# Second gated MLP: the first block product copied by ScalarE into a second PSUM bank, and new due times for the planner

## The chip, the cores and the metric

The kernel runs on one core of a Trainium2 chip. The metric is the device time of one execution in microseconds. Of three runs of the kernel before, the median is 1006.6 us (1005.06 to 1008.88); the execution that was profiled took 1006.01 us, with a span of 1004.2 us from its first to its last instruction.

## The reference, cut to what matters

Attention over 4 batches of 576 tokens with 8 heads of 64 (half of the heads see a plain window of 32, half a dilated one) is followed by two gated MLPs on 2304 tokens, 512 wide inside and 1536 in the middle:

```python
def _moe_ref(x, w_gate, w_val, w_out, rms_g):        # first MLP
    xn = x / np.sqrt(np.mean(x * x, -1, keepdims=True) + 1e-06) * rms_g
    g = xn @ w_gate
    return g * (1.0 / (1.0 + np.exp(-g))) * (xn @ w_val) @ w_out

def _moe2_ref(x, w_gate, w_val, w_out):              # second MLP
    gate = 1.0 / (1.0 + np.exp(-(x @ w_gate)))
    return gate * (x @ w_val) @ w_out
```

## The kernel before, in words

Every fp32 product is made of three passes of TensorE on a high and a low part of each operand (high by high, high by low, low by high); `split` (line 578) makes the parts: a cast on ScalarE, a subtraction on GpSimd or VectorE.

The order of all work is planned in Python while the kernel is built. `add` enters an operation with its engine (or engines, each other one at a penalty from `PARAMS`), its cost, what it reads and writes, its tiles and a due time. `Line.emit` then plays the engines forward: each engine takes the operation that can begin first, and among those that can begin at once the one with the smallest due time. A tile of a ring (a PSUM bank, a buffer) can be taken when its last user has ended. Each engine then runs its list in the order found. Products of the two MLPs carry the key `PE order`, so TensorE keeps the order in which they were entered; what the planner chooses for them is the time. The due times come from `PARAMS`: `att0`, `span0` and `lo1` to `hi5` for the attention groups, `turn0` and `turn1` for the first transposes, `wdue` and `wslope` for the weights of the first MLP, and so on.

Stages: attention of the first tokens, then chunks of 384 tokens of the first MLP in which the remaining attention is interleaved (to about 280 us of the profile), the rest of the first MLP (to about 588 us), the second MLP, and the output.

The second MLP (`half`, `unit`, `y_products`) multiplies 2x2 blocks with seven block products in place of eight (Winograd's form): four blocks of the result, named 11, 12, 21, 22, are sums of seven products. Three passes hold four of the twelve column groups each; a pass goes over four batches, a batch over two units, a unit has a gate half and a value half: 24 units, 48 halves, seven products of six matmuls each. In a half, product 0 goes to bank X and ScalarE copies it to SBUF as block 11 (`snap`, line 1595); product 1 goes to Y and is copied as block 22; product 2 is added by TensorE onto X and copied as block 12; product 3 is added onto Y and VectorE adds Y to 12 (`plus`, line 1601); product 4 is added onto X, and VectorE adds X to 22; product 5 goes to bank Z and VectorE adds Z to 11; product 6 is added onto X, which then is block 21. `finish` (line 1607) takes a tanh of a gate block on ScalarE (line 1612) or multiplies a value block by its gate on VectorE (line 1624). Block 21 is read from its bank, the other three from SBUF. The two halves of a unit take turns product by product.

Banks: X takes `g`, `v` and `y3` in turn; Y and Z take the two banks `att`. The output products of the batch before (`y_products`, line 1487) are put between, at places given by `y_from` and `y_step` (`y_last` in the last batch but one); their X is `y0` or `y1` in turn, Y and Z are `y2`. Each ends in an addition on VectorE (line 1463). Outputs go out through transposes on VectorE (line 1560) and four DMAs each (line 1567); the last two pairs of blocks through transposes on TensorE into `g` and `v` (line 1539), copies on ScalarE (line 1544) and DMAs (line 1551).

Of the kernel before, what the change touches and what calls it, by code (L numbers as in the profile page):

```python
# [8 lines left out]
F32 = mybir.dt.float32  # L9
# [15 lines left out]
    "late": 0, "fill_share": -1.519, "fill_max": 6, "gather": 0.866, "w0_hi": 17.594,  # L25
    "w0_lo": 13.068, "h0_hi": 0.512, "h0_lo": -0.096, "x0_hi": 0.96, "x0_lo": 1.138, "ahead": 2,
    "todo0": 464.368, "todo1": 9.635, "todo2": 47.212, "todo3": 0.618, "xb_zero": -1.082,
    "stay": 0.104, "phase": 1.6, "fill_from": 7.028, "fill_gap": -3.039, "margin": 2139.515,
    "wait": 1.172, "w_sq": 3.146, "w_hi": 0.024, "w_lo": 0.907, "x_hi": 0.265, "x_lo": 0.0,
    "h_hi": 7.774, "h_lo": 0.002, "qk": 0.304, "norm": 0.51, "pts": 8.696, "o": 0.0, "snap": 6.738,  # L30
    "h_ahead": 8.667, "h2_ahead": 0.956, "evac": 7.026, "holds": (6, 6), "norm_act": 1.016,
    "slack": 0.0, "share_v": 0.6, "share_p": 0.33, "cold": 1.7, "low": 0, "high": 0.39,
    "recip": 0.3, "rel1": 106.122, "span1": -0.902, "rel2": 17.835, "span2": -0.521, "ys": 0.468,
    "ts": 0.415, "cross": 0.06, "same": 0.04, "dma_lat": 1.7, "dma_rate": 330000.0, "by_pe": 0,
# [3 lines left out]
    "ld_v": -61.445, "ld_c": -66.281, "ld_d": -14.37, "lead": 1.181, "xdue": 12.095,  # L38
    "wdue": -1.028, "wslope": 2.786, "wload": -341.212, "wload_step": 9.03, "warm_n": 36,
    "warm_t": 0.889, "warm_dt": 0.03, "warm_c": 19, "warm_m": 5, "warm_late": -3.526,  # L40
    "warm_due": 32.425, "mask_cost": 0.18, "exp_cost": 0.36, "s_cost": 0.546, "o_cost": 0.41,
    "t_cost": 0.265, "pt_lead": 8.027, "x_lead": 12.171, "wy_due": -0.031, "y_from": 7.985,
    "y_step": 1.502, "xb_due": 0.362, "y_last": 1.346, "xb_last": 6.045, "lo6": 114.359,
    "hi6": 18.752, "sizes": (384, 384, 384, 384, 384, 384), "wide": (384, 384, 384, 384, 384, 384),
    "rush": -0.629, "rush_to": 0.301,
# [296 lines left out]
def attention_then_two_gated_mlps(  # L342
# [103 lines left out]
    def act(n):  # L446
        return 0.09 + n / 1190
# [589 lines left out]
    def x_norm(c, due, banks):  # L1037
        T1 = SIZES[c]
        R = T1 // TT
        sq = new("sb", "pt", [P, KD, T1], F32, 2)  # L1040
# [72 lines left out]
        xo = [new("sb", "xo", [P, 2, 2, T1], F32R, NX) for _ in range(2)]  # L1113
        rbp = new("ps", banks[1], [P, TT, R], F32, 2 if banks[1] == "att" else 1)

        def turn():
# [3 lines left out]
        add("PE", 0.247, turn, reads=[("rb", c), "ident"], writes=[("rbp", c), "x order"],  # L1120
            tiles=[rb, rbp] + xo, due=due, lat=0.08, cols=3 * R, fill=filler(rbp))
        xtile[0, c] = xo
        for kk in range(KD):
# [14 lines left out]
            if L2P > ONE:  # L1138
                dma(lambda kk=kk, xn=xn: nc.sync.dma_start(out=xf_scr[c][:, kk], in_=xn.t),
                    512.0 * T1, reads=[("xn", c, kk)], writes=[("xf", c, kk)], tiles=[xn],  # L1140
                    due=due + 12)
        for k in range(2):
# [154 lines left out]
    def mlp_step(p, c, f, s):  # L1297
# [11 lines left out]
        def proj(which, bank, due):  # L1309
            def products(ks):  # L1310
                for kk in ks:
# [3 lines left out]
                    for n, (l, r) in enumerate(((0, 0), (0, 1), (1, 0))):  # L1315
# [3 lines left out]
                                         start=kk == 0 and n == 0, stop=kk == KD - 1 and n == 2)  # L1319

            alone = (p, c, f, which) == (0, 0, 0, 0)
            for ks in [[kk] for kk in range(KD)] if alone else [list(range(KD))]:
# [6 lines left out]
                    cols=3 * T1 * len(ks), fill=filler(bank) if ks[0] == 0 else None)  # L1329

        proj(0, gb, s)
        if p:
            add("ACT", act(T1), lambda: nc.scalar.activation(out=t.t, in_=gb.t, func=ACTF.Silu),
                reads=[("bank", p, c, f, 0)], writes=[key], tiles=[gb, t], due=s + 1.9 * mul)
        else:
# [8 lines left out]
            writes=[key], tiles=[vb, t], due=s + 3.7 * mul)  # L1344
# [523 lines left out]
```

## Time and profile before

| | |
|---|---|
| median of three runs | 1006.6 us (1005.06 to 1008.88) |
| the profiled execution | 1006.01 us, span 1004.2 us |
| TensorE busy | 977.1 us, 97% of the span |
| VectorE busy | 732.2 us, 73% |
| ScalarE busy | 477.8 us, 48% |
| GpSimd busy | 406.3 us, 40% |
| mean granted TensorE clock | 0.975 of full |
| HBM | 129.5 MB read, 63.7 MB written |

How to read it: PE is TensorE's matmuls, PEld its weight loads, DVE VectorE, ACT ScalarE, POOL GpSimd, SP the engine that issues DMAs. A granted clock of 1.00 is 2.4 GHz, 0.50 is 1.2 GHz. A busy TensorE with clock 1.00 in a long stretch is a stretch that is bound by its own products; what can be won or lost there are gaps. The idle time named for a group is that of its engine just before it, with what ended the wait.

### The profile page before, as it was taken

To read this page: it belongs to the slowest core of one execution; us is meant where nothing else is said; L and a number is where in the kernel's file an instruction comes from. 1 tells how busy PE (TensorE), PEld (TensorE's weight loads), DVE (VectorE), ACT (ScalarE), POOL (GpSimd) and SP (SyncE) were. 2 spreads that over 40 slices of the span, in tenths; PEclk is the share of its full clock that TensorE was granted. 3 is DMA by queue.
4 is the path that set the end of the run, shared out by engine and by line. 5 is a ranking of instruction groups with operands and counts; after the bars stand their busy time and mean duration, and the time that the engine had idled before them with its cause. 6 is when DMAs were issued, how large, how long until landed. Compare 5 with 4: busy or idle time off the path is not lost. (4 is left out here: it accounts for less than half of the span.)

```text
span 1004.2 us, 20084 instructions
## 1 busy us (share of the span) xinstructions
PE 977.1 (97%) x7096; PEld 947.2 (94%) x7096; DVE 732.2 (73%) x1712; ACT 477.8 (48%) x1305; POOL 406.3 (40%) x602
## 2 busy tenths in 40 slices
PE   7899899999999999999999999999999999999997
PEld 6688798998999999999999999999999999999996
DVE  6778897868895888733432579788977688787765
ACT  5876657647442542322221345646654446454432
POOL 5653874444342730010000467337852047651111
PEclk8769799999999999999999999999999999999998
DMA  9858698676779587966563354645176454547634
GB/s 203 190 154 178 136 287 218 156 201 198 250 226 364 193 285 236 345 204 219 214 216 101 107 168 180 237 166 184 66 255 224 155 199 147 202 134 217 160 85 87
DMA packets 213253, 194.53 MB, mean 194 GB/s; under 512 B 137313, under 2 KB 178849, under 8 KB 213153
## 3 DMA queue, kind: packets, MB, share of 16 engines
q1 hardware_dynamic: 213152, 193.25, 63.5%
q8 instruction: 56, 0.92, 0.4%
q14 instruction: 45, 0.36, 0.1%
HBM read 129.50 MB, written 63.70 MB: 192 GB/s over the span
## 5 line engine op out<-in xcount | busy, mean ns | idle before, releaser
L1368 PE MATMUL y<-h,wo 128*128 128x384 f32 x864 | 166.5, 338 | 0.5 <-DVE h L588 0.4
L1318 PE MATMUL g<-xo,w 128*128 128x384 f32 x864 | 165.9, 340 | 0.0
L1318 PE MATMUL v<-xo,w 128*128 128x384 f32 x864 | 163.0, 336 | 0.0
L1318 PEld LDWEIGHTS g<-xo,w 128*128 128x128 f32 x864 | 152.2, 191 | 0.4 <-issue 0.2
L1368 PEld LDWEIGHTS y<-h,wo 128*128 128x128 f32 x864 | 149.3, 188 | 2.4 <-DVE h L588 0.7
L1318 PEld LDWEIGHTS v<-xo,w 128*128 128x128 f32 x864 | 150.4, 188 | 1.3
L581 ACT CAST h<-t 128x384 fp32r<-128x384 f32 (+1 forms) x139 | 65.8, 473 | 116.7 <-DVE t L1342 87.3
L585 POOL TENSOR_TENSOR h<-t,h 128x288 fp32r<-128x288 f32 (+1 forms) x45 | 42.8, 953 | 159.3 <-ACT h L581 153.4
L1463 DVE SCALAR_TENSOR_TENSOR pt<-y,pt 128x288 f32<-128x288 f32 x136 | 61.3, 451 | 37.2 <-PE y L1510 34.5
L1342 DVE TENSOR_TENSOR t<-t,v 128x384 f32<-128x384 f32 x72 | 39.6, 549 | 66.0 <-PE v L1318 65.4
L972 POOL TENSOR_SCALAR pr<-pr,rs 128x96 f32<-128x96 f32 x132 | 57.0, 445 | 57.0 <-DVE rs L967 39.5
L1510 PE MATMUL y<-h,wo 128*128 128x288 f32 x408 | 75.0, 298 | 0.1
L588 DVE TENSOR_TENSOR h<-t,h 128x384 fp32r<-128x384 f32 (+1 forms) x95 | 58.8, 619 | 20.5 <-ACT h L581 19.6
L585 POOL TENSOR_TENSOR w<-wz,w 128x256 fp32r<-128x256 f32 x58 | 47.5, 833 | 46.3 <-ACT w L581 32.9
L562 ACT ACTIVATE wz<-wst 128x512 f32<-128x512 f32 x72 | 48.0, 670 | 33.4 <-DMA z<-wz 21.5
L1510 PEld LDWEIGHTS y<-h,wo 128*128 128x128 f32 x408 | 61.4, 190 | 0.8 <-DVE pt L1463 0.3
L585 POOL TENSOR_TENSOR w<-S,w 128x256 fp32r<-128x256 f32 x48 | 38.7, 820 | 52.1 <-DVE w L583 38.0
L571 DVE SCALAR_TENSOR_TENSOR wz<-wst,wz 128x512 int32<-128x512 int32 x72 | 56.6, 787 | 0.9
L959 ACT ACTIVATE pr<-pr,nmx 128x96 f32<-128x96 f32 x144 | 52.4, 365 | 9.2 <-DVE nmx L953 8.9
L574 DVE SCALAR_TENSOR_TENSOR wz<-wst,wz 128x512 int32<-128x512 int32 x72 | 52.8, 734 | 0.6
L1612 ACT ACTIVATE t<-t 128x288 f32<-128x288 f32 x72 | 31.9, 444 | 44.7 <-DVE t L1603 43.2
L585 POOL TENSOR_TENSOR x<-t,x 128x288 fp32r<-128x288 f32 x29 | 27.2, 940 | 63.0 <-ACT x L581 62.9
(224 smaller groups left out, 2111.4 us busy)
## 6 DMA issues: line engine op xcount, KB each, us to landing
z<-wz SPq DMA_DIRECT2D x54, 256.0 KB, 4.4
xo<-xs SPq DMA_DIRECT2D x23, 576.0 KB, 5.8
wst<-in_moe_w_gate_dram SPq DMA_DIRECT2D x24, 512.0 KB, 4.6
wst<-in_moe_w_val_dram SPq DMA_DIRECT2D x24, 512.0 KB, 5.1
wst<-in_moe_w_out_dram SPq DMA_DIRECT2D x24, 512.0 KB, 5.5
xs<-xs SPq DMA_DIRECT2D x21, 576.0 KB, 2.8
wst<-xs SPq DMA_DIRECT2D x18, 576.0 KB, 5.4
x<-xo SPq DMA_DIRECT2D x24, 384.0 KB, 3.2
```

The lines of the kernel that those rows point to most:

```text
L562: add("ACT", act(CW), lambda: nc.scalar.activation(out=z.t.bitcast(F32), in_=top().bitcast(F32), func=ACTF.Abs), reads=[("wst", key)], wri ...
L571: add("DVE", Shared(0.595), lambda: nc.vector.scalar_tensor_tensor(out=z.t, in0=top(), scalar=-0x40000000, in1=z.t, op0=ALU.bitwise_and, o ...
L574: add("DVE", Shared(0.595), lambda: nc.vector.scalar_tensor_tensor(out=z.t, in0=low(), scalar=29, in1=z.t, op0=ALU.logical_shift_right, op ...
L581: add("ACT", act(n), lambda: nc.scalar.copy(out=hi(), in_=src()), reads=reads, writes=[key] + [order] * bool(order), tiles=tiles + [dst], ...
L585: add("PL", pool(n), lambda: nc.gpsimd.tensor_tensor(out=lo(), in0=src(), in1=hi().bitcast(F32), op=ALU.subtract), reads=reads, writes=[ke ...
L588: other=(kind + "_lo", "DVE", dves(n), lambda: nc.vector.tensor_tensor(out=lo(), in0=src(), in1=hi().bitcast(F32), op=ALU.subtract)))
L959: add("ACT", PARAMS["exp_cost"], lambda u=u: nc.scalar.activation(out=pr.t[:, u], in_=pr.t[:, u], func=ACTF.Exp, bias=nmx.t[:, u:u + 1], s ...
L972: add("PL", Shared(0.305), lambda u=u: nc.gpsimd.tensor_scalar(out=pr.t[:, u], in0=pr.t[:, u], scalar1=rs.t[:, u:u + 1], scalar2=1.0, op0= ...
L1318: nc.tensor.matmul(out=bank.t, lhsT=w[:, l, cols], rhs=x, start=kk == 0 and n == 0, stop=kk == KD - 1 and n == 2)
L1368: nc.tensor.matmul(out=yb.t, lhsT=w.t[:, l, s], rhs=hs[r].t if broad(p, c) else hs[r].t[:, r], start=n == 0 and j == 0, stop=n == HOLDS[p] ...
L1463: add("DVE", dve(T), lambda: nc.vector.scalar_tensor_tensor(out=t.t[:, e, h], in0=bank.t, scalar=0.5, in1=t.t[:, e, h], op0=ALU.mult, op1= ...
L1510: nc.tensor.matmul(out=bank.t, lhsT=w.t[:, u, a, n], rhs=hs[u].t[:, d], start=first and u == 0 and m == 0, stop=u == NF // 2 - 1 and m == ...
```

## The change

In each half of the second MLP, `fork` copies product 0 from X into bank Z (ScalarE, PSUM to PSUM) where `snap` had copied it to SBUF, and product 5 is added by TensorE onto Z. Block 11 is then complete in Z and is read from there; the addition `plus("11", ...)` on VectorE is gone. Product 6 (block 21) is now made ahead of product 5 (block 11), in the halves and in the output products. Banks: X and Z are `g` and `y0` in the gate half, `v` and `y1` in the value half, Y takes the two `att`; output products use `y2` as X and `y3` as Y and Z, in the last batch separate banks. The transposes for the last rows go to `att`. Nearly all due times and penalties in `PARAMS` are new. Code that `raw0` would switch on is added, with `raw0` at 0; a Silu in place of a tanh is added for passes of the first MLP in this form, and there are none (`L2P == ONE`).

```diff
-    "h_ahead": 8.667, "h2_ahead": 0.956, "evac": 7.026, "holds": (6, 6), "norm_act": 1.016,
+    "h_ahead": 10.342, "h2_ahead": 0.492, "evac": 7.728, "holds": (6, 6), "norm_act": 1.104,
...
-    "turn0": 0.86, "turn1": -186.059, "turn2": -12.842, "att0": -231.169, "span0": 205.466,
-    "lo1": 1.867, "hi1": 22.152, "lo2": 3.699, "hi2": 43.659, "lo3": 43.617, "hi3": 74.163,
-    "lo4": 77.56, "hi4": 111.875, "lo5": 139.429, "hi5": 93.074, "ld_a": -87.98, "ld_b": -134.366,
+    "turn0": -7.478, "turn1": -224.953, "turn2": -8.055, "att0": -127.647, "span0": 115.808,
+    "lo1": -0.631, "hi1": 22.322, "lo2": 2.971, "hi2": 44.131, "lo3": 39.592, "hi3": 63.762,
+    "lo4": 53.961, "hi4": 86.73, "lo5": 105.105, "hi5": 51.067, "ld_a": -72.708, "ld_b": -80.637,
...
-    "wdue": -1.028, "wslope": 2.786, "wload": -341.212, "wload_step": 9.03, "warm_n": 36,
+    "wdue": -1.768, "wslope": 2.791, "wload": -1142.697, "wload_step": 21.266, "warm_n": 36,
...
-    "t_cost": 0.265, "pt_lead": 8.027, "x_lead": 12.171, "wy_due": -0.031, "y_from": 7.985,
-    "y_step": 1.502, "xb_due": 0.362, "y_last": 1.346, "xb_last": 6.045, "lo6": 114.359,
+    "t_cost": 0.265, "pt_lead": 1.167, "x_lead": 0.604, "wy_due": -2.854, "y_from": 5.481,
+    "y_step": 1.405, "xb_due": -1.663, "y_last": 1.961, "xb_last": -0.797, "lo6": 19.514,
...
@@ def y_products(p, b):
-        steps = (("X", (("11", 1, 0),)), ("Y", (("22", 1, 0),)), ("X", (("12", 1, 0),)),
-                 ("Y", (("12", 0, 1),)), ("X", (("22", 0, 1),)), ("Z", (("11", 0, 1),)),
-                 ("X", (("21", 1, 1),)))
+        steps = ((0, "X", (("11", 1, 0),)), (1, "Y", (("22", 1, 0),)), (2, "X", (("12", 1, 0),)),
+                 (3, "Y", (("12", 0, 1),)), (4, "X", (("22", 0, 1),)), (6, "X", (("21", 1, 1),)),
+                 (5, "Z", (("11", 0, 1),)))
...
-                    for key, tag in zip("XYZ", (f"y{y_count[0] % 2}", "y2", "y2")):
+                    tags = ("y2", "y3", "y3")
+                    if (p, b) == (LAST, LAST_B):
+                        tags = (("y2", "y3", "y0"), ("g", "v", "y1"))[n]
+                    for key, tag in zip("XYZ", tags):
...
@@ def out_rows(b, n, h, t0, nt, due):
-        bank = new("ps", "vg"[out_count[0] % 2], [TQ, nt, 2, P], F32, 1)
+        bank = new("ps", "att", [TQ, nt, 2, P], F32, 2)
...
@@ def half(p, b, u, f, which, uk, X, Y, Z, gate, square):
-        c = {name: one_of(T_HOMES, [P, T]) for name in ("11", "12", "22")}
+        c = {name: one_of(T_HOMES, [P, T]) for name in ("22", "12")}
         ck = {name: ("c", name, uk) for name in c}
-        ck["21"] = ("X", uk)
+        ck["21"], ck["11"] = ("X", uk), ("Z", uk)
+        of_bank = {"21": X, "11": Z}
...
+        def fork(at):
+            add("ACT", act(T), lambda: nc.scalar.copy(out=Z.t, in_=X.t), reads=[("X", uk)],
+                writes=[("Z", uk)], tiles=[X, Z], due=at - PARAMS["snap"])
...
-            s = X if name == "21" else c[name]
+            s = of_bank.get(name) or c[name]
...
-        steps = (("X", lambda at: snap("11", X, "X", at)),
-                 ("Y", lambda at: snap("22", Y, "Y", at)),
-                 ("X", lambda at: snap("12", X, "X", at)),
-                 ("Y", lambda at: (plus("12", Y, "Y", at), finish("12", at))),
-                 ("X", lambda at: (plus("22", X, "X", at), finish("22", at))),
-                 ("Z", lambda at: (plus("11", Z, "Z", at), finish("11", at))),
-                 ("X", lambda at: finish("21", at)))
+        steps = ((0, "X", fork),
+                 (1, "Y", lambda at: snap("22", Y, "Y", at)),
+                 (2, "X", lambda at: snap("12", X, "X", at)),
+                 (3, "Y", lambda at: (plus("12", Y, "Y", at), finish("12", at))),
+                 (4, "X", lambda at: (plus("22", X, "X", at), finish("22", at))),
+                 (6, "X", lambda at: finish("21", at)),
+                 (5, "Z", lambda at: finish("11", at)))
...
@@ def unit(p, b, u, at, extra):
-            X = new("ps", ("g", "v", "y3")[bank_count[0] % 3], [P, T], F32, 1)
-            bank_count[0] += 1
-            Z, Y = (new("ps", "att", [P, T], F32, 2) for _ in range(2))
+            X, Z = (new("ps", tag, [P, T], F32, 1) for tag in (("g", "y0"), ("v", "y1"))[which])
+            Y = new("ps", "att", [P, T], F32, 2)
```

## Rows read from the trace of the kernel before

**Rows 1.** The page's first part: busy time of each engine, share of the span.

```profile
PE 977.1 (97%) x7096; PEld 947.2 (94%) x7096; DVE 732.2 (73%) x1712; ACT 477.8 (48%) x1305; POOL 406.3 (40%) x602
```

**Rows 2.** Windows: length, busy of PE, PEld, DVE, ACT, POOL, clock, DMA, GB/s.

```profile
0.00:125.00 125.00, 108.12 (x1002) 93.54 (x1003) 97.03 (x358) 87.45 (x303) 75.79 (x164) 0.82 0.78 172
100.00:125.00 25.00, 20.33 (x178) 18.15 (x177) 21.36 (x71) 16.73 (x57) 22.06 (x40) 0.80 0.63 132
125.00:300.00 175.00, 173.52 (x1404) 162.15 (x1403) 147.30 (x410) 99.67 (x299) 83.29 (x160) 1.00 0.77 220
600.00:975.00 375.00, 373.67 (x2806) 372.29 (x2805) 297.78 (x598) 189.37 (x500) 172.64 (x196) 1.00 0.54 175
975.00:1004.20 29.20, 22.26 (x143) 19.97 (x142) 18.28 (x42) 7.44 (x17) 5.86 (x8) 0.91 0.39 82
```

**Rows 3.** Windows of the half-clock stretches, and their sum (five windows).

```profile
46.40:66.90 20.50, 18.85 (x167) 15.83 (x168) 15.75 (x68) 14.60 (x54) 11.30 (x23) 0.50 0.45 92
114.70:124.90 10.20, 8.29 (x58) 7.65 (x55) 9.12 (x36) 6.67 (x24) 9.36 (x20) 0.50 0.42 106
985.10:988.50 3.40, 3.40 (x14) 2.94 (x13) 1.92 (x5) 0.86 (x2) 0.80 (x1) 0.50 0.61 173
...
sum 47.80, PE 43.00 PEld 37.23 DVE 34.87 ACT 32.16 POOL 29.81; mean PE 8.60 PEld 7.45 DVE 6.97 ACT 6.43 POOL 5.96
```

**Rows 4.** Waits of PE, 760 to 975 us: who for whom, total, times, longest.

```profile
PE att L1586 <- ACT t L1597: 0.7, 1, 0.7
PE g L1586 <- ACT t L1612: 0.4, 1, 0.4
```

**Rows 5.** Single lines: count, duration ns min/median/max, first and last start.

```profile
L1603 DVE TENSOR_TENSOR t<-t,att x96: 408/443/456, 594.8 to 979.4; 128x288 f32<-128x288 f32 x96
L1603 DVE TENSOR_TENSOR t<-t,g x16: 436/444/455, 596.5 to 956.6; 128x288 f32<-128x288 f32 x16
L1597 ACT COPY t<-att x48: 391/400/415, 590.5 to 967.8; 128x288 f32<-128x288 f32 x48
```

**Rows 6.** Groups by line and shape, 605 to 985 us: busy us, mean ns, idle before.

```profile
L1624 DVE SCALAR_TENSOR_TENSOR t<-t,t 128x288 f32<-128x288 f32 x65 | 41.8, 644 | 3.5 <-ACT t L1612 1.2
L1624 DVE SCALAR_TENSOR_TENSOR t<-t,y 128x288 f32<-128x288 f32 x8 | 3.6, 446 | 0.4 <-PE y L1586 0.4
```

**Rows 7.** Timeline, 842 to 848 us: start, length, engine, line, idle before.

```profile
842.57 0.96 PE L1586 MATMUL g<-xq,w 128*128 128x288 f32 x6
...
846.28 0.43 ACT L581 CAST h<-t 128x288 fp32r<-128x288 f32 x1 [1.96 <-DVE t L1187]
846.62 0.41 ACT L1612 ACTIVATE t<-g 128x288 f32<-128x288 f32 x1
...
847.07 1.05 PE L1586 MATMUL g<-xo,w 128*128 128x288 f32 x6 [0.38 <-ACT t L1612]
```

**Rows 8.** Timeline of PE, second MLP's first unit: two products one after the other.

```profile
597.48 0.96 PE L1586 MATMUL g<-xo,w 128*128 128x288 f32 x6
598.28 0.96 PE L1586 MATMUL v<-xo,w 128*128 128x288 f32 x6
```

**Rows 9.** Timeline of the end, 980 to 1004 us, the rows of PE and SP.

```profile
980.24 0.96 PE L1586 MATMUL y<-xq,w 128*128 128x288 f32 x6
...
981.75 0.40 PE L1510 MATMUL y<-pt,wo 128*128 128x288 f32 x1 [0.15 <-ACT pt L581]
...
982.63 0.53 PE L1510 MATMUL y<-pt,wo 128*128 128x288 f32 x2 [0.48 <-POOL pt L585]
...
983.77 0.40 PE L1510 MATMUL y<-pt,wo 128*128 128x288 f32 x1 [0.22 <-ACT pt L581]
...
984.65 0.54 PE L1510 MATMUL y<-pt,wo 128*128 128x288 f32 x2 [0.48 <-POOL pt L585]
...
989.62 8.92 SPq L1567 DMA_DIRECT2D out_dram<-ob  x16
...
998.64 3.04 SPq L1551 DMA_DIRECT2D out_dram<-wz  x4
```

More of the change, by code (lines that the diff above doesn't have):

```diff
@@ L24 @@
 PARAMS = {
[L25 to L30, printed above, removed]
@@ L40 @@
[L40 to L45 removed]
+    "late": 0, "fill_share": -1.399, "fill_max": 6, "gather": 0.305, "w0_hi": 13.595,
@@ L1039, in x_norm @@
         R = T1 // TT
+        raw = not c and PARAMS["raw0"]
+        if raw:
+            plain_split(due)
         sq = new("sb", "pt", [P, KD, T1], F32, 2)
@@ L1112, in x_norm @@
                 writes=[("rb", c)], tiles=[ssp, ms, a, y, rb], due=due)
-        xo = [new("sb", "xo", [P, 2, 2, T1], F32R, NX) for _ in range(2)]
+        xo = xtile[0, 0] if raw else [
+            new("sb", "xo", [P, 2, 2, T1], F32R, NX) for _ in range(2)]
         rbp = new("ps", banks[1], [P, TT, R], F32, 2 if banks[1] == "att" else 1)
@@ L1118, in turn @@
                 nc.tensor.transpose(rbp.t[:, t], rb.t[:, t], ident[0:R, 0:R])
-        add("PE", 0.247, turn, reads=[("rb", c), "ident"], writes=[("rbp", c), "x order"],
-            tiles=[rb, rbp] + xo, due=due, lat=0.08, cols=3 * R, fill=filler(rbp))
+        add("PE", 0.247, turn, reads=[("rb", c), "ident"], writes=[("rbp", c)] + ["x order"] * (not raw),
+            tiles=[rb, rbp] + ([] if raw else xo), due=due, lat=0.08, cols=3 * R, fill=filler(rbp))
+        if raw:
+            row = rowtile[0] = new("at", "row", [P, T1], F32, 1)
+            add("ACT", act(T1), lambda: nc.scalar.copy(
+                out=row.t, in_=rbp.t.rearrange("p t o -> p (t o)")), reads=[("rbp", c)],
+                writes=["row"], tiles=[rbp, row], due=due,
+                other=("ys", "DVE", dve(T1), lambda: nc.vector.tensor_copy(
+                    out=row.t, in_=rbp.t.rearrange("p t o -> p (t o)"))))
+            dma(lambda: nc.sync.dma_start(out=row_scr, in_=row.t), rows(P, 4 * T1), reads=["row"],
+                writes=["row out"], tiles=[row], due=due + 12)
+            x_store(c, xo, due)
+            return
         xtile[0, c] = xo
@@ L1318, in products @@
                         nc.tensor.matmul(out=bank.t, lhsT=w[:, l, cols], rhs=x,
-                                         start=kk == 0 and n == 0, stop=kk == KD - 1 and n == 2)
+                                         start=kk == order[0] and n == 0,
+                                         stop=kk == order[-1] and n == 2)
             alone = (p, c, f, which) == (0, 0, 0, 0)
-            for ks in [[kk] for kk in range(KD)] if alone else [list(range(KD))]:
+            order = KK_FIRST if alone and PARAMS["raw0"] else range(KD)
+            for ks in [[kk] for kk in order] if alone else [list(range(KD))]:
                 add("PE", 3 * mm(T1) * len(ks), lambda ks=ks: products(ks),
@@ L1344, in mlp_step @@
             writes=[key], tiles=[vb, t], due=s + 3.7 * mul)
+        if raw:
+            add("PL", pool(raw), lambda: nc.gpsimd.tensor_tensor(
+                out=t.t[:, 0:raw], in0=t.t[:, 0:raw], in1=row.t, op=ALU.mult),
+                reads=[("row", "rowm")[p]], writes=[key], tiles=[t, row], due=s + 3.7 * mul,
+                other=("x0_lo", "DVE", dves(raw), lambda: nc.vector.tensor_tensor(
+                    out=t.t[:, 0:raw], in0=t.t[:, 0:raw], in1=row.t, op=ALU.mult)))
         if broad_:
@@ L1439, in part_load, with row_load @@
                 due=due)
+    def row_load(due):
+        t = rowtile[1] = new("mid", "row", [P, SIZES[0]], F32, 1)
+        dma(lambda: nc.sync.dma_start(out=t.t, in_=row_scr), rows(P, 4 * SIZES[0]),
+            reads=["row out"], writes=["rowm"], tiles=[t], due=due)
     def sums_load(p, b, n, due):
@@ L1468, in sum_part @@
         if p == LAST and (b, n) == (LAST_B, 1):
-            if (e, h) in ((1, 1), (1, 0)):
+            if (e, h) in ((1, 1), (0, 0)):
                 for t0, nt in ((0, 2), (2, 1)):
@@ L1473, in sum_part @@
             out_blocks(b, n, e, h, due)
-        elif (e, h) == (1, 0) and p == L2P - 1:
+        elif (e, h) == (0, 0) and p == L2P - 1:
             for i in range(2):
@@ L1782, in whole @@
                     if p and not fi:
+                        if p == 1 and not c and PARAMS["raw0"]:
+                            row_load(s - 20)
                         x_load(p, c, s - 25)
```

94 lines of the change are left out of this document (67 added, 27 removed).

## The prediction

> **What bounds the kernel now.** I read the page's busy shares first, then windows by stage, then the granted clock, then who TensorE waits for, and the timeline of the end. TensorE is busy 97% of the span, VectorE 73% [rows 1]. By stage [rows 2]: from 600 to 975 us, which is the second MLP but for its ends, TensorE is busy 373.67 of 375 us at full clock, so it loses 1.33 us there; from 125 to 300 us it loses 1.48 us. VectorE is busy 297.8 of those 375 us. What is lost lies at the two ends. Before 125 us TensorE sits idle 125 - 108.1 = 16.9 us and works at half clock in four stretches of together 47.8 - 3.4 = 44.4 us with 43.0 - 3.4 = 39.6 us of work in them [rows 3], which at full clock would take half: 19.8 us. After 975 us it is idle about 7 us, with one more stretch of half clock. So the second MLP is bound by its own products: 48 halves and 24 sets of output products, seven products each, 504 in all, begin 0.80 us apart [rows 8]. The change leaves that number as it is.
>
> **Part 1: one addition less in each half.** The addition takes 0.443 us [rows 5]; there are 96 + 3 x 16 = 144, three in each of 48 halves, so 48 go: 21.3 us of VectorE. In addition, the 24 value multiplications of block 11 now read a bank. With both operands in SBUF one takes 644 ns, with one in a bank 446 ns [rows 6]: 24 x 0.198 = 4.8 us less. Together 26.1 us, from 297.8 to about 272 us in the long window. All of it lies beside TensorE, which waits in that window only 1.33 us. So the 26 us themselves are worth nothing, and only those 1.33 us of stalls can be got back. The two that I can name are 0.70 and 0.38 us long, and in both ScalarE was late [rows 4]; in the second it stood idle for 1.96 us behind a cast that waited for VectorE, while its tanh on the bank could have run [rows 7]. A lighter VectorE shortens that kind. I take -1.0 us; the lower end is -1.3, the upper end is the rival of the banks below.
>
> The Trainium skill, Perfetto Trace Analysis (Optimizing Scalar/DVE Operations), says the opposite of the rows on one point: a VectorE operation pays more to reach PSUM (about 125 ns) than SBUF (about 60 ns). By that figure the multiplication of block 11 would become 65 ns dearer, 24 x 0.065 = 1.6 us more where I count 4.8 us less, an estimate from that page. The measured 446 against 644 ns decides here; the sum is the same either way, and VectorE would be relieved by 19.7 us in place of 26.1, which weighs a little for the rival of the banks.
>
> **Part 2: the copy into a bank.** 48 copies from bank to SBUF, 400 ns each [rows 5], become copies from bank to bank. No row shows ScalarE writing a bank; the nearest are this copy, 391 ns at its fastest [rows 5], and a cast within SBUF, 430 ns [rows 7]. Between these, 48 copies move ScalarE by -0.4 to +1.4 us of its 189.4 us in the window [rows 2]; I take the copy's own 400 ns, so 0, hidden either way. What counts is what the copy waits for: bank Z of the unit before, hence in the value half the last multiplication of that unit on VectorE. Behind it on ScalarE stand the copies of Y and X. Cover: block 11 is finished by the last product of a unit, and the copy must be ready for product 2 of the next unit, five products or 4.0 us later, with output products between up to 5.6 us. Two operations of 0.45 and 0.40 us have to fit in that. Value taken 0.
>
> **Part 3: other banks and another order of products.** X of the gate half is asked for again three products (2.4 us) after its last product where no output product lies between, and about 4 us after where two do. Before, three banks took turns. For output products, X was `y0` or `y1` in turn and is now always `y2`: between its last product and the next first one lie one output product and about 2.8 half products (`y_step` is 1.405, two sets), some 3.0 us, for one addition of 0.45 us. Both are covered as long as the readers start within about 2 us. Value 0, with the price in the rivals.
>
> **Part 4: the end.** Output products are put in at 5.481 + 1.961 i of the last batch's 28 half products; i = 12 and 13 fall beyond 28. So two output products, 1.6 us, stand behind the last unit, where before all 14 were in by 7.985 + 13 x 1.346 = 25.5. There TensorE now waits 0.15 + 0.48 + 0.22 + 0.48 = 1.33 us for the operands of the last unit [rows 9], and right behind it runs 3.40 us at half clock [rows 3]. Against this: block 11 comes last now. Before, two products (1.6 us), an addition (0.44) and a multiplication (0.64) put it 0.5 us ahead of the end of the halves, now one multiplication puts it 0.45 us behind it, 1.0 us later. So the waits shrink by 1.6 - 1.0 = 0.6 us, to 0.7 us. A wait of 0.70 us in the window before did not lower the clock [rows 2, 4], so I take the half-clock stretch as gone: half of 3.40, 1.7 us. Together -2.3 us. The ends: -3.0 (all waits gone too) and +1.0 (block 11 late, clock as before). The output DMAs could hide the gain: SP issues 16 of them in 8.92 us without a pause, and only then those of the last rows [rows 9]. They begin when the first block of the last batch is ready, though, and that moves with TensorE.
>
> The Trainium skill, TensorE: Matmul & The Clock Gate (Part 1: The HAM clock gate), has the same mechanism: the engine falls to half clock after it has been idle and regains it by working. By the trace it fell right behind these waits and nowhere else after 125 us, which agrees. The page adds that the point at which this happens shifts from run to run; by that the 1.7 us could come or go in any one execution.
>
> **Part 5: new due times elsewhere.** Two due times matter only against each other. Before 125 us the order is nearly as it was: the loads keep their rank (-134, -88, -66, -61, -14 becomes -81, -73, -69, -62, -15), the first attention groups stay ahead of all weights, and those of the second chunk go from 1.9 to -0.6 against weights that go from -1.0 to -1.8. What moves far is the attention of the last three chunks (`hi5` from 93 to 51, `lo4` from 78 to 54). It lies where TensorE loses 1.48 us in 175 [rows 2], so nothing is to be won there. I take 0. But a plan drawn anew can meet the start otherwise. The nearest price is its last gap: from 100 to 125 us TensorE is idle 4.67 us [rows 2], and 114.7 to 124.9 us is at half clock with 8.29 us of work [rows 3], 4.1 us too many. Together 8.8 us, to be won if it closes, to be lost if another like it opens. Code behind `raw0` and the Silu is not built: 0.
>
> **The sum** goes against the profiled execution, 1006.0 us (1004.2 of span and 1.8 around it): -1.0 - 2.3 = -3.3, so 1002.7 us. That execution lies 0.6 us under the median of 1006.6; the three runs are 3.8 us apart, so I don't correct for it. About 0.5%, 5.0 us, is what a measurement can tell from no change: faster is below 1001.6, slower above 1011.6.
>
> **The rivals.**
> A, the start closes. The gap between the first chunk and the second goes, 8.8 us or a good part: 994 to 998 us. For it: 36.7 us are lost in the start, far more than elsewhere. Against: the relative order there hardly changes.
> B, the start opens: another gap with a half-clock stretch, 1007 to 1014 us, around 1011.5. For it: VectorE and GpSimd are busy 21.4 and 22.1 of 25 us in that gap, so a little more work at the wrong place is late at once. Against: as for A.
> C, the banks stall TensorE, slower. Place: X of the gate half at each change of unit. In the trace the tanh on bank `g` began 846.62 - 843.53 = 3.1 us after its product, and TensorE, which wanted the bank after 3.2 us, waited 0.38 [rows 7]. With 2.4 us of cover such a lag costs 0.38 + 0.76 = 1.1 us. It decides from a lag of about 2 us on; if half of 24 units had it, 13 us: some 1015 us. For it: no third bank any more, and ScalarE runs a fixed list. Against: two waits of this kind in 215 us [rows 4], and a VectorE with 26 us less.
> D, the gain is hidden: stalls and clock at the end come out as they are, 1006 us, whatever VectorE saves.
>
> **How the numbers follow.** Forecast 0.46, with 999.7 to 1005.7 as its own range, a third of it (0.16) below 1001.6; A 0.24; B 0.12, half of it slower; C 0.08; D 0.10. Faster 0.16 + 0.24 = 0.40; within 0.5% 0.30 + 0.06 + 0.10 = 0.46; slower 0.06 + 0.08 = 0.14. The range 994 to 1011.5 leaves out the far side of A (0.06), the upper half of B and C.
>
> **What would show it.** Right: 96 additions in place of 144 in the second MLP, VectorE near 272 us in 375; TensorE's waits there under 1 us in total; no wait for a half's bank over 0.5 us; two output products behind the last unit and no half clock after 125 us; idle time and half clock before the second chunk within 3 us of 16.9 and 44.4. Wrong: TensorE waits of several us on ScalarE or VectorE at changes of unit (C), or a start whose idle time and half clock differ by a stretch (A, B).

## The result and the profile after

The changed kernel took 1012.57 us, median of four runs (1011.78 to 1014.64); the kernel before, four runs beside it on the same chip, 1006.83 us. The ratio is 1.0071, 95% interval [1.0047, 1.0096]: slower, and 1.07 us above the range that was forecast. The profiled execution of the changed kernel took 1011.78 us, with a span of 1010.0 us.

First the page's busy shares after the change, to be read against [rows 1]:

```profile
PE 976.5 (97%) x7096; PEld 947.0 (94%) x7096; DVE 715.3 (71%) x1711; ACT 473.8 (47%) x1293; POOL 389.5 (39%) x567
```

Every engine but TensorE has less to do, and the span is 5.8 us longer. The windows by stage, with columns as in [rows 2]; the last one is the end:

```profile
0.00:125.00 125.00, 106.86 (x998) 93.18 (x999) 97.54 (x358) 87.82 (x301) 74.16 (x160) 0.81 0.80 174
...
125.00:300.00 175.00, 172.87 (x1402) 162.22 (x1401) 141.22 (x405) 95.15 (x295) 87.80 (x162) 1.00 0.73 208
600.00:975.00 375.00, 371.60 (x2785) 369.70 (x2784) 290.16 (x598) 187.21 (x485) 140.44 (x156) 1.00 0.53 173
975.00:1010.00 35.00, 26.37 (x181) 23.80 (x179) 23.44 (x53) 7.19 (x18) 5.09 (x6) 1.00 0.41 91
```

The first two are within 1.3 us of before. In the second MLP TensorE now loses 3.40 us of 375, where it lost 1.33, and VectorE, which was to fall to 272 us, is at 290.16. The half-clock stretch near the end is gone: the granted clock is 1.00 to 1010.

Cut at the first product of the second MLP, the end of its halves and the end of the span, the two traces read (us):

| | before | after |
|---|---|---|
| first product of the second MLP | 587.9 | 588.2 |
| from there to the last product of a half | 393.3 | 395.7 |
| from there to the end | 23.0 | 26.1 |

Three output products (3 x 0.80 us) have moved from the second line to the third: 17 stand behind the last product of a half where 14 stood before. The first of the three was put in at 5.481 + 1.961 x 11 = 27.05, so it follows the 28th half product too. They are products 4, 6 and 5 of a set; the last two half products, product 4, and the start of product 6 (start and duration in us, then engine, line and operation; in brackets the idle time before it and what ended it):

```profile
982.13 1.75 PE L1658 MATMUL y<-xq,w 128*128 128x288 f32 x12
983.73 0.97 PE L1586 MATMUL y<-h,wo 128*128 128x288 f32 x6
985.47 0.66 PE L1586 MATMUL y<-pt,wo 128*128 128x288 f32 x3 [0.78 <-DVE pt L1540]
```

With the three taken out, the halves are 2.4 + 2.4 = 4.8 us longer, the end is 3.1 - 2.4 = 0.7 us longer, and what lies ahead 0.3 us. That is all of the 5.8 us.

Who TensorE waited for in the halves (587 to 984 us; us in total, times, longest), against the named waits before, which are the two of [rows 4] and one more:

```profile
PE g L1658 <- DVE t L1679: 3.6, 4, 1.4
PE y L1586 <- DVE pt L1540: 0.5, 1, 0.5
PE v L1658 <- DVE t L1679: 0.3, 1, 0.3
```

The one more, in the kernel before, where line 1586 is a half's product and line 1612 the tanh:

```profile
PE y L1586 <- ACT t L1612: 0.2, 1, 0.2
```

And at the end (984 to 1010 us), against the operand waits of [rows 9]:

```profile
PE y L1586 <- DVE pt L1540: 1.4, 2, 0.8
PE att L1612 <- DVE pt L1540: 1.1, 2, 0.6
PE g L1586 <- DVE pt L1540: 0.9, 1, 0.9
PE y L1586 <- POOL pt L585: 0.5, 1, 0.5
PE y L1586 <- POOL h L585: 0.5, 1, 0.5
...
```

In the changed kernel line 1658 is a half's product, 1679 the addition `plus`, 1586 an output product, 1540 its addition on VectorE, 1612 a transpose of the last rows. The waits for ScalarE's tanh are gone. In their place TensorE waits for VectorE's additions, in front of banks `g` and `v`, which are now X. The first such wait is in the first unit, where no output product lies between. The timeline:

```profile
593.10 0.43 DVE L703 TENSOR_TENSOR S<-wz 128x256 f32<-128x256 f32 x1 [4.15 <-DMA wz<-z]
...
594.85 1.06 PE L1658 MATMUL g<-xo,w 128*128 128x288 f32 x6
...
595.86 1.05 PE L1658 MATMUL v<-xo,w 128*128 128x288 f32 x6
...
597.54 0.45 DVE L1679 TENSOR_TENSOR t<-t,g 128x288 f32<-128x288 f32 x1
...
598.04 1.06 PE L1658 MATMUL g<-xo,w 128*128 128x288 f32 x6 [1.12 <-DVE t L1679]
```

The two rows at 594.85 and 595.86 are product 4 of the gate and of the value half; the next product on `g` is product 6. It must not touch `g` until VectorE has added it to block 22. The cover for that is the one product on `v` between: 0.8 us. The addition began 1.6 us after product 4 had ended, and TensorE stood for 1.12 us. VectorE came late because the head of its list had waited 4.15 us for a DMA of weights, until 593.10; sums of these weights and the operations listed behind them then ran almost without a pause. In the kernel before, it waited 3.18 us there, until 591.83, and the addition ended 1.7 us behind its product, inside the cover of three products. The longest wait, although output products lie between there, with VectorE's queue in front of it:

```profile
858.51 0.96 PE L1658 MATMUL g<-wst,w 128*128 128x288 f32 x6
...
859.88 0.44 DVE L1679 TENSOR_TENSOR t<-t,att 128x288 f32<-128x288 f32 x1
...
860.25 0.41 DVE L661 TENSOR_TENSOR S<-wz,S 128x256 f32<-128x256 f32 x1
...
860.59 0.99 DVE L1697 SCALAR_TENSOR_TENSOR t<-t,t 128x288 f32<-128x288 f32 x1
...
861.50 0.95 DVE L661 TENSOR_TENSOR S<-wz 128x256 f32<-128x256 f32 x1
...
862.37 0.45 DVE L1540 SCALAR_TENSOR_TENSOR pt<-y,pt 128x288 f32<-128x288 f32 x1
...
862.74 0.44 DVE L1679 TENSOR_TENSOR t<-t,g 128x288 f32<-128x288 f32 x1
...
863.23 0.93 PE L1658 MATMUL g<-xq,w 128*128 128x288 f32 x5 [1.38 <-DVE t L1679]
```

Product 4 on `g` ended at 859.47. The other addition (`att`, 859.88) and four operations without haste (two sums of weights, a multiplication, an output sum) then ran ahead of the addition that TensorE waited for, which began at 862.74. In the kernel before product 5 of both halves lay between too: three products, 2.4 us. Over the 48 halves the median time from the end of product 4 to the start of product 6, output products and stalls included, is 3.82 us before and 2.04 after; the addition ends up to 3.1 us behind its product before, and up to 3.7 after.

### The profile page after: what moved, and what is told of

Same layout as the page of the kernel before. It is cut to its first block, busy times and chain, and to the rows that moved or that the text cites. A ratio compares the mean times of both kernels' runs of the same rounds, so it can differ in the third digit from the quotient of the medians.

```text
span 1010.0 us, 19990 instructions
## 1 busy us (share of the span) xinstructions
PE 976.5 (97%) x7096; PEld 947.0 (94%) x7096; DVE 715.3 (71%) x1711; ACT 473.8 (47%) x1293; POOL 389.5 (39%) x567
## 4 chain that ended last, share of the span: by engine, by line
PE 80%; DVE 9%; DMA 4%; POOL 2%; ACT 2%; issue 2%; SPq 1%; POOLq 0%; DVEq 0%; ACTq 0%
PE g L1360 13%; PE v L1360 13%; PE y L1440 13%; PE y L1586 11%; PE v L1658 6%; PE g L1658 6%; PE att L1658 6%; PE y L1658 3%; PE att L941 3%; DMA wz<-z 2%; PE att L999 1%; PE att L986 1%; DMA xo<-in_k_dram 1%; DVE wz L568 1%; DVE wz L571 1%
## 5 line engine op out<-in xcount | busy, mean ns | idle before, releaser
L1440 PEld LDWEIGHTS y<-h,wo 128*128 128x128 f32 x864 | 149.4, 188 | 1.4
L585 POOL TENSOR_TENSOR h<-t,h 128x288 fp32r<-128x288 f32 (+1 forms) x35 | 34.1, 976 | 147.1 <-ACT h L581 147.1
L1540 DVE SCALAR_TENSOR_TENSOR pt<-y,pt 128x288 f32<-128x288 f32 x130 | 58.7, 452 | 34.0 <-PE y L1586 33.5
L588 DVE TENSOR_TENSOR h<-t,h 128x384 fp32r<-128x384 f32 (+1 forms) x105 | 67.5, 644 | 20.2 <-ACT h L581 19.6
L1586 PE MATMUL y<-h,wo 128*128 128x288 f32 x396 | 72.5, 296 | 1.3 <-DVE pt L1540 0.6
L1586 PEld LDWEIGHTS y<-h,wo 128*128 128x128 f32 x396 | 59.1, 188 | 2.0 <-DVE pt L1540 0.9
L1399 ACT ACTIVATE t<-g 128x384 f32<-128x384 f32 x36 | 17.7, 493 | 86.1 <-PE g L1360 86.1
L585 POOL TENSOR_TENSOR xs<-xq,xs 128x576 fp32r<-128x576 f32 x16 | 23.8, 1488 | 83.7 <-ACT xs L581 76.4
L1229 DVE TENSOR_TENSOR t<-t,t 128x288 f32<-128x288 f32 x85 | 46.4, 545 | 7.9 <-POOL h L585 2.7
```

The lines of the kernel that those rows point to most:

```text
L585: add("PL", pool(n), lambda: nc.gpsimd.tensor_tensor(out=lo(), in0=src(), in1=hi().bitcast(F32), op=ALU.subtract), reads=reads, writes=[ke ...
L588: other=(kind + "_lo", "DVE", dves(n), lambda: nc.vector.tensor_tensor(out=lo(), in0=src(), in1=hi().bitcast(F32), op=ALU.subtract)))
L1440: nc.tensor.matmul(out=yb.t, lhsT=w.t[:, l, s], rhs=hs[r].t if broad(p, c) else hs[r].t[:, r], start=n == 0 and j == 0, stop=n == HOLDS[p] ...
L1540: add("DVE", dve(T), lambda: nc.vector.scalar_tensor_tensor(out=t.t[:, e, h], in0=bank.t, scalar=0.5, in1=t.t[:, e, h], op0=ALU.mult, op1= ...
L1586: nc.tensor.matmul(out=bank.t, lhsT=w.t[:, u, a, n], rhs=hs[u].t[:, d], start=first and u == 0 and m == 0, stop=u == NF // 2 - 1 and m == ...
```

## The experiments

Each run was compared with runs of the kernel before on the same chip. "Second MLP" is the time from its first product to the end of the span in the profiled execution: 416.3 us before, 421.8 after. "Waits" are TensorE's named waits in the halves: 1.3 us before, 4.4 after. Two limits: each kernel was profiled in one execution only, and the change itself (1.0071) was not run again beside its variants, so a ratio of a variant is compared with it by way of the kernel before, and differences of 0.2 to 0.3% between such ratios lie inside their intervals.

**The order of products 5 and 6 put back, in the changed kernel**: in the halves, in the output products, in both.

```diff
-                 (6, "X", lambda at: finish("21", at)),
-                 (5, "Z", lambda at: finish("11", at)))
+                 (5, "Z", lambda at: finish("11", at)),
+                 (6, "X", lambda at: finish("21", at)))
```

> The changed kernel with the old order of products in the halves alone: product 5 (bank Z) again ahead of product 6 (bank X). Everything up to the second MLP is planned as in the changed kernel. Theory 1 (order): product 6 right behind product 4 leaves VectorE too little time to add X to block 22, so the waits of TensorE for VectorE's addition in the halves (5.5 us lost in ten of them between 588 and 984 us, product starts against 0.80 us each) fall below 1.5 us, and the time falls by 3 to 5 us from 1012.6 to about 1008.5. Theory 2 (due times): the new due times put the additions late; then the waits stay near 5 us and the time within 1 us of 1012.6. Theory 3 (copy into the bank): ScalarE's copy and the bank Z hold TensorE up; the waits stay as well.

> The changed kernel with the old order of products 5 and 6 in the output products alone. Theory 1 (order): in the halves the waits stay (5.5 us); at the end, where output products follow one another without half products between, the waits for VectorE's sums (0.94, 0.78 and 1.08 us, and 0.67 us at 744 us) lose 1.5 to 2.5 us in all; the time falls by 1 to 2.5 us to about 1011. Theories 2 and 3: the waits at the end stay, the time within 1 us of 1012.6.

> The old order in halves and output products; copy into the bank, banks and due times stay as changed. Theory 1: the two gains add up, 4.5 to 7 us, about 1006.5, that is within 1.5 us of the kernel before. Theory 2 (due times) and theory 3 (copy): at most 1 us faster than 1012.6.

Measured: halves 1.009 [1.0057, 1.0123], second MLP 424.3 us; output products 1.0062 [1.0043, 1.0081], 419.9 us; both 1.0138 [1.0105, 1.017], 427.6 us. The old order brought nothing back. The waits of the first and the last, with the columns of the waits above:

```profile
PE g L1658 <- ACT t L1690: 3.2, 6, 1.2
PE y L1586 <- DVE pt L1540: 0.5, 1, 0.5
```

```profile
PE v L1658 <- DVE t L1697: 3.7, 2, 2.2
PE g L1658 <- ACT t L1690: 2.5, 2, 1.3
PE g L1658 <- DVE t L1679: 0.5, 1, 0.5
```

With the old order the waits for line 1679 are nearly gone, so the order did cause them. But block 21 is then the last product of X and must leave its bank (tanh, line 1690, or multiplication, line 1697) before the next unit's first product: the stall has moved to the change of unit. That is the place of the rival of the banks. There is no third X bank there any more: Z takes `y0` and `y1`, and the output products have moved to `y2` and `y3`.

**The two halves of the cause, each alone in the kernel before**: two X banks in place of three; product 6 ahead of product 5.

```diff
-            X = new("ps", ("g", "v", "y3")[bank_count[0] % 3], [P, T], F32, 1)
+            X = new("ps", ("g", "v")[bank_count[0] % 2], [P, T], F32, 1)
...
-            for i, (key, then) in enumerate(steps)]
...
+            for i in (0, 1, 2, 3, 4, 6, 5)]
```

> The kernel before with one edit: bank X of the halves takes g and v in turn, without the third bank y3. No copy into a bank, old order, old due times. Theory 4 (banks): the third X bank is what the new kernel lost by giving each half a Z of its own, and its loss costs TensorE waits whatever the order of products; without it, product 0 of the next unit waits for the tanh or the multiplication of block 21, at 8 or more of 24 changes of unit, 3 to 6 us in all, and the time rises by 0.3 to 0.8% over the kernel before. Theory 2 (due times) and theory 3 (copy into the bank): no more than 1 us lost in halves beyond what the kernel before loses (1.7 us), ratio within 0.998 to 1.003.

> The kernel before with one edit: in the halves product 6 (bank X) is made ahead of product 5 (bank Z), as in the change; three X banks, no copy into a bank, old due times. Theory 1 (order): product 6 right behind product 4 waits for VectorE's addition of X to block 22; 3 to 6 us lost in the halves between 588 and 984 us, ratio 1.003 to 1.007. Theory 4 (banks) expects part of it too, since the order shortens the cover of the same bank from 2.4 to 0.8 us. Theory 3 (copy): nothing, ratio within 0.998 to 1.002.

Measured: two banks 1.0059 [1.0035, 1.0082], second MLP 419.4 us, waits 3.1 us; the order 1.0171 [1.0133, 1.021], 430.4 us, waits 9.5 us. Their waits:

```profile
PE g L1586 <- ACT t L1612: 2.1, 4, 1.2
PE v L1586 <- DVE t L1624: 1.0, 3, 0.6
```

```profile
PE y L1586 <- DVE t L1603: 6.0, 3, 2.9
PE y L1586 <- ACT t L1597: 1.7, 1, 1.7
PE g L1586 <- DVE t L1603: 1.1, 2, 1.0
...
```

In this kernel line 1586 is the half's product, 1603 the addition, 1612 the tanh. Each half of the cause slows the old kernel, the order by far more than either theory said (it also worked 5.98 us at half clock in the halves). With the order alone VectorE still has all its 144 additions, and the waits are twice those of the change.

**The copy into the bank left out**: in the changed kernel block 11 goes to SBUF again and VectorE adds.

```diff
...
-        steps = ((0, "X", fork),
+        steps = ((0, "X", lambda at: snap("11", X, "X", at)),
...
-                 (5, "Z", lambda at: finish("11", at)))
+                 (5, "Z", lambda at: (plus("11", Z, "Z", at), finish("11", at))))
...
```

> The changed kernel without its copy into the bank: product 0 is copied to SBUF again, product 5 starts bank Z afresh and VectorE adds Z to block 11 (144 additions). Order, banks and due times as in the change. Theories 1 and 4 (order, banks): the waits for VectorE at product 6 stay or grow, since VectorE has 21 us more to do; ratio to the kernel before 1.006 to 1.013. Theory 3 (copy): the waits go, ratio 1.003 or less.

Measured: 1.0153 [1.0113, 1.0192], second MLP 427.3 us; TensorE waits 6.9 us for line 1679 where the change waits 3.9. So the copy into the bank is the good part, worth some 0.8% under this order, these banks and these due times: what slows the kernel is what came with it.

**Due times**: the change with the old `PARAMS`; the kernel before with the new.

> The changed kernel with all due times and penalties of the kernel before; order, copy and banks as changed. Theory 1 (order): TensorE's waits for VectorE's additions in the halves stay, 3 us or more lost between 588 us and the end of the halves, and the time stays above 1009. Theory 2 (due times): these waits fall below 1.5 us and the time returns to 1007 or less. Theory 3 (copy): as theory 1, but the waits are for ScalarE.

> The kernel before with all due times and penalties of the change; old order, banks, no copy into a bank. Theory 2 (due times): the loss is there, ratio 1.005 to 1.010. Theory 4 (banks) and theory 1 (order): halves lose less than 2.5 us to waits; what the due times do to the start is within 3 us, ratio 0.997 to 1.003.

Measured: 1.0084 [1.0054, 1.0115], 422.7 us; 1.0089 [1.0057, 1.012], 421.8 us. The old due times don't rescue the change, and the new ones by themselves cost the old kernel as much as the change does. The latter was the miss for my theory that only banks and order count. Its waits are few:

```profile
PE att L1586 <- DVE t L1603: 2.1, 1, 2.1
PE g L1586 <- ACT t L1612: 0.4, 1, 0.4
```

Most of its loss is clock: 3.41 us of work at half clock after the first wait, and at the end this window (columns as above):

```profile
988.00:998.20 10.20, 9.27 (x34) 8.31 (x35) 7.08 (x15) 1.73 (x4) 2.70 (x4) 0.50 0.43 96
```

Half of 3.41 + 9.27 is 6.3 us, against 1.7 us in the kernel before: 4.6 us more. TensorE's idle time grew too, from 1.33 to 2.48 us in the halves and from 1.57 to 3.78 us behind them. Together that is more than the 5.5 us that were lost, so the shares are rough.

**The addition served first**: the additions of `plus` due 20 us earlier; then the same with the output order put back.

```diff
-                writes=[ck[name]], tiles=[bank, t], due=at)
+                writes=[ck[name]], tiles=[bank, t], due=at - 20)
```

> The changed kernel with the two additions left on VectorE (blocks 12 and 22) due 20 us earlier, so that VectorE takes them ahead of everything else that is ready. Order, banks and copy as changed. Theory 5 (the cover of X is short, and VectorE comes late because other work is due before the addition): the waits of TensorE for these additions in the halves fall from 5.5 us to 2 us or less, the second MLP from its first product to the end takes 418 to 420 us in place of 421.8, ratio to the kernel before 1.001 to 1.005. Rival (VectorE is late because an operation of up to 1 us is already running, or because its list is simply full): the waits stay at 4 us or more, ratio 1.005 to 1.009.

> The same earlier additions, and the old order of products 5 and 6 in the output products alone (in the run with that alone the second MLP took 419.9 us). Theory 5: both gains, 416 to 418.5 us for the second MLP to the end, ratio 0.998 to 1.003. Rival: 419.5 us or more, ratio 1.004 or more.

Measured: 1.0045 [1.0025, 1.0064], 418.4 us, waits 2.7 us, 2.1 of them for the additions: as theory 5 expected, but for 0.1 us of the waits; with the output order 1.0052 [1.0031, 1.0073], 419.5 us, which adds nothing. After the first:

```profile
PE g L1658 <- DVE t L1679: 2.1, 2, 1.1
PE y L1586 <- DVE pt L1540: 0.6, 1, 0.6
```

The order of VectorE's queue was thus 3.4 us of the loss in the profiled executions, where the waits of line 1679 fell from 3.9 to 2.1 us; by the ratios it was 2.6 us, but the two intervals overlap. What stays is the first unit (1.1 us), where 0.8 us of cover meets an addition that stands behind the late weights whatever its rank, one wait of 1.0 us in the second unit, and the end.

**The end**: two output products behind the last unit in the kernel before; none in the changed one.

```diff
-    "y_step": 1.502, "xb_due": 0.362, "y_last": 1.346, "xb_last": 6.045, "lo6": 114.359,
+    "y_step": 1.502, "xb_due": 0.362, "y_last": 1.7, "xb_last": 6.045, "lo6": 114.359,
...
-    "y_step": 1.405, "xb_due": -1.663, "y_last": 1.961, "xb_last": -0.797, "lo6": 19.514,
+    "y_step": 1.405, "xb_due": -1.663, "y_last": 1.405, "xb_last": -0.797, "lo6": 19.514,
```

> The kernel before with y_last 1.7 in place of 1.346: two output products of the last batch but one stay behind the last unit, as in the change, and nothing else differs until the last batch. If the two products cover the operands of the last unit, as part 4 of the prediction had it: the waits of 1.33 us there and the half-clock stretch behind them go, 1.5 to 3 us faster, ratio 0.997 to 0.9985. Rival (the work for the operands is limited by VectorE and GpSimd and by the sums of these two products themselves): within 1 us of the kernel before, waits still 1 us or more.

> The changed kernel with y_last 1.405 in place of 1.961: all 14 output products are put in before the last unit ends, none is left behind it. Block 11 now comes last with nothing to cover it: by part 4 of the prediction the waits for the operands of the last unit grow by about 1.5 us and a half-clock stretch follows, 1.5 to 3 us slower than the changed kernel, ratio 1.008 to 1.011. Rival (the two products behind the last unit cover nothing): the same within 1 us, ratio 1.006 to 1.008.

Measured: 1.0024 [1.0002, 1.0045], 416.9 us; 1.0074 [1.0045, 1.0104], 420.4 us. The change has three products there, not two as these expectations have it. What Part 4 had expected came out in neither kernel: two products behind the last unit gain nothing in the old kernel, and taking the change's three away costs nothing that can be told from noise. In the old one they came with 6.17 us of work at half clock in place of 3.40.

**Is it VectorE's load?** With the new penalties GpSimd makes fewer subtractions and VectorE more: line 588 has 103 instructions of together 62.9 us from 600 to 975 us, before 79 of 46.9 us. Two kernels take that load away and serve the addition first: one with the old `PARAMS`, one with the new due times and low penalties for GpSimd.

```diff
-    "wait": 4.071, "w_sq": 11.208, "w_hi": 0.214, "w_lo": 1.683, "x_hi": 1.928, "x_lo": 0.111,
-    "h_hi": 36.337, "h_lo": 0.0, "qk": 1.674, "norm": 0.246, "pts": 4.965, "o": 0.0, "snap": 4.37,
+    "wait": 4.071, "w_sq": 11.208, "w_hi": 0.024, "w_lo": 0.907, "x_hi": 0.265, "x_lo": 0.0,
+    "h_hi": 7.774, "h_lo": 0.4, "qk": 1.674, "norm": 0.246, "pts": 4.965, "o": 0.0, "snap": 4.37,
...
-    "ts": 9.224, "cross": 0.06, "same": 0.04, "dma_lat": 1.7, "dma_rate": 330000.0, "by_pe": 0,
+    "ts": 0.415, "cross": 0.06, "same": 0.04, "dma_lat": 1.7, "dma_rate": 330000.0, "by_pe": 0,
```

> The change with the due times and penalties of the kernel before, and VectorE's additions of X to blocks 12, 21 and 22 due 20 us earlier. Theory 5 with the handed-back relief (the new penalties put 24 more subtractions on VectorE, 103 for 79, and so keep its additions late): with the old penalties VectorE is busy about 283 us of 375 in the second MLP, the additions come sooner still, waits of the half products at or below 2.0 us, 2nd MLP 417 to 418.5 us, ratio 0.999 to 1.004. Rival (the penalties don't matter, what is left is the order 4, 6 itself in the first unit and at the end): waits as with the new penalties, 2.1 to 2.7 us, ratio 1.004 to 1.007.

> The change with its additions due 20 us earlier, and with the penalties for GpSimd's subtractions set low, so that VectorE makes about half as many of them over the whole run. Theory of the handed-back relief: VectorE is busy 275 to 283 us of 375, waits at or below 2.0 us, 2nd MLP 417 to 418.5 us, ratio 0.999 to 1.004. Rival (the order alone): 2.1 to 2.7 us of waits, ratio 1.004 to 1.007; or GpSimd's longer subtractions come late for products and for the start, ratio above 1.007.

Measured: 1.0068 [1.0042, 1.0094] and 1.0073 [1.0047, 1.0099], second MLP 421.5 and 420.5 us. The second one's windows, its waits in the halves, and its half-clock window:

```profile
600.00:975.00 375.00, 373.34 (x2803) 372.16 (x2802) 273.39 (x533) 184.88 (x479) 209.11 (x243) 1.00 0.52 174
...
991.90:1002.10 10.20, 8.77 (x34) 7.98 (x34) 4.29 (x10) 0.86 (x2) 1.54 (x2) 0.50 0.42 96
```

```profile
PE g L1658 <- DVE t L1679: 1.3, 1, 1.3
PE y L1586 <- DVE pt L1540: 0.8, 2, 0.5
...
```

VectorE is where Part 1 had put it, 273 us (282 in the first of the two), and one wait for the addition is left: the first unit's, 1.3 us, as long as ever. So load is not what keeps that one: the order does (with the old order it was gone), together with the weights that come late. Both kernels missed the 1.004 or less that the theory of load had expected. The kernel is no faster for it, because its end waits as that of the change does, and then works 8.77 us at half clock (4.4 us lost; 9.16 us of work in the first kernel). No version beat the kernel before.

## Why the prediction was wrong, point by point

**What bounds the kernel: right.** The second MLP is bound by its own products, so VectorE's relief had nothing to win but small stalls.

**Part 1: the count right, the relief and its gain not.** Single lines of the change, 600 to 975 us and around (min/median/max ns):

```profile
L1679 DVE TENSOR_TENSOR t<-t,att x48: 416/443/456, 595.9 to 976.8; 128x288 f32<-128x288 f32 x48
L1679 DVE TENSOR_TENSOR t<-t,g x24: 439/443/455, 597.5 to 978.3; 128x288 f32<-128x288 f32 x24
L1679 DVE TENSOR_TENSOR t<-t,v x24: 437/452/457, 597.9 to 979.1; 128x288 f32<-128x288 f32 x24
```

96 additions, as forecast, and multiplications with a bank operand at 451 ns on average against 615 with both in SBUF (groups by form, 605 to 985 us: busy us and mean ns, then idle time before them):

```profile
L1697 DVE SCALAR_TENSOR_TENSOR t<-t,t 128x288 f32<-128x288 f32 x41 | 25.2, 615 | 2.2
L1697 DVE SCALAR_TENSOR_TENSOR t<-t,y 128x288 f32<-128x288 f32 x22 | 9.9, 451 | 5.9 <-PE y L1658 4.8 <-ACT pt L581 0.9
```

But 16 of the 26 us went back to VectorE as subtractions, through the new penalties, which the prediction had not looked at. And the two stalls that were to shrink made way for longer ones.

**Part 2: right.** Copies from bank to bank:

```profile
L1674 ACT COPY y<-g x24: 383/383/394, 589.2 to 968.8; 128x288 f32<-128x288 f32 x24
L1674 ACT COPY y<-v x24: 357/383/391, 590.0 to 969.5; 128x288 f32<-128x288 f32 x24
```

383 ns where 400 was assumed, and no wait of TensorE names line 1674.

**Part 3: the step that failed.** It said "Both are covered as long as the readers start within about 2 us. Value 0". It measured the time between two uses of X only at the change of unit and between sets of output products. Inside the half, product 6 directly behind product 4 leaves 0.8 us where there had been 2.4 us, and the reader between them, `plus("22")`, ends 0.84 us behind its product in the median, but up to 3.7 us. With Part 1's stalls, the halves were to shrink by 1.0 us and grew by 4.8, of which 3.4 went when the addition was served first. The price that the rival of the banks had (0.38 to 1.1 us for each late reader) was of about the right size (0.3 to 1.4 us), its place was not: the tanh that it named is no longer waited for.

**Part 4: wrong by 3.0 us** (-2.3 forecast, +0.7 measured). It counted two output products behind the last unit and there are three, which by its own working would have covered more. The half-clock stretch went, as said, but the waits, which were to fall from 1.33 to 0.7 us, rose: idle time from the end of the halves to the last output product went from 1.57 to 4.21 us. The working had operands arriving late. Operands are late as before (0.5 + 0.5 + 0.2 + 0.2 us for lines 585 and 581). What is new is waits for VectorE's sums of the output products in front of a bank (line 1540). In two of them, 1.4 us on `y`, product 6 follows product 4 on one bank as in the halves, here with nothing between. Another 1.1 us are the last transposes, which read these sums (0.6 us before). The remaining 0.9 us, on `g`, has another origin: there product 4 waits for the sum of product 2, with product 3 between, and VectorE's list is again held up at its head, by a transpose that waited for an output DMA:

```profile
999.90 0.48 DVE L1633 STREAM_TRANSPOSE ob<-pt 128x288 f32<-128x288 f32 x1 [1.19 <-DMA out_dram<-ob]
1000.30 0.42 DVE L1540 SCALAR_TENSOR_TENSOR pt<-g,pt 128x288 f32<-128x288 f32 x1
...
1000.77 0.66 PE L1586 MATMUL g<-x,wo 128*128 128x288 f32 x3 [0.92 <-DVE pt L1540]
```

That the order is to blame for the loss at the end was not shown: putting it back in the output products alone gave 0.09% at most, inside the intervals. The run with y_last at 1.7 shows that two products behind the last unit bring no gain by themselves.

**Part 5: right for the start, incomplete.** The first product of the second MLP came at 587.9 and 588.2 us. Over the profiled executions that share the plan up to there it lies at 587.5 to 592.0 with the old due times and at 587.5 to 592.5 with the new: the same to within the scatter. So neither rival A nor B. But the new due times by themselves cost the old kernel 0.9%, in the second MLP, a place that the step did not look at.

What stays open is the half clock at the end. Behind the stalls there the clock fell in 12 of the 16 profiled kernels, and did not in four, the change with its 4.21 us of idle time among them. The Trainium skill, TensorE: Matmul & The Clock Gate (Part 1: The HAM clock gate), says that the point at which the clock changes shifts from one run to the next. No run here shows whether that decides, since each kernel was profiled once; the mean granted clock of the kernel before did range from 0.972 to 0.985 over 29 executions on one chip. Which of the new due times brings it on in the old kernel was not tried.

## What to carry to other kernels

Where products are put in another order, write down for every bank each pair of neighbouring uses, with the reader that must be through between them and the products that cover it: the smallest cover decides, and here it fell from 2.4 to 0.8 us inside the loop while the change of unit looked safe. An engine with less work is not an engine that answers sooner; what counts is what stands ahead of the urgent operation in its queue, and giving that one priority won back 3.4 of 5.5 us in the profiled executions. What the head of its list waits for counts as well: a late DMA there held up everything behind it. When a plan's penalties change with the structure, run each alone: here either one without the other is slower than the kernel that neither touched.

## What the runs showed of the hardware that was not expected

- ScalarE's copy from bank to bank (383 ns) is no dearer than from bank to SBUF (400 ns) for 128x288 fp32, and TensorE's later products add onto what ScalarE wrote there.
- A few idle microseconds at the end often cost as much again in clock, but not each time: 3.92 us of idle at the end of one kernel came with 8.8 us of work at half clock, so 4.4 us lost, 3.73 us in another (the order of the halves put back) with 2.9 us of work, so 1.4 us lost, and 4.21 us in the changed kernel with none.
- The value multiplications with both operands in SBUF were long where GpSimd worked beside them: in the kernel before, those that ran while GpSimd was idle took 456 ns on average (25 of 72), those with its work beside them for over half of their length 808 ns (38). With one operand in a bank it was 445 ns either way. So nearly all of the 0.198 us that Part 1 counted for each goes with GpSimd's work, not with the place of the operand alone.
- Profiled executions whose plan is the same up to the second MLP reach it up to 4.5 us apart with the old due times and 5.0 us with the new. Loss inside a stage had to be measured from the start of that stage; against the whole time it would have been lost in this scatter.
